# Six weight blocks transposed by DMA instead of TensorE and VectorE, in a kernel whose order of work is a written table

## Chip, core and metric

The kernel runs on one core of a Trainium2 chip. The metric is the device time of one launch in microseconds (us): the median of three runs before the change is 213.56 us (213.39 to 213.92). The engines of a core work side by side and meet only through semaphores: TensorE (PE in the profile), VectorE (DVE), ScalarE (ACT), GpSimd (POOL), and SyncE (SP), which here issues nearly all the DMAs.

## Reference, cut to what matters

Chunk-selecting attention over 4 batches of 8 heads (768 positions, 64 per head), followed by a gated MLP block with a matrix `w_sg` (768x768) that mixes positions:

```python
h = x @ w_in                                   # x: attention's output, 768 x 512 per batch
h = gelu(h)
u, v = h[..., :512], h[..., 512:]
v_n = (v - mean(v)) / sqrt(var(v) + 1e-6) * g_ln
v_s = einsum('ts,bsd->btd', w_sg, v_n) + b_sg[None, :, None]
return x + (u * v_s) @ w_out
```

The sum over `s` needs `w_sg` with `s` on the partitions, that is, transposed.

## The kernel before, in words

`_build` makes a list of steps with `P.op` (lines 57 to 98): each has an engine, a function that emits its instructions, an estimated cost, the names that it reads and writes, and a tag. Dependencies follow from the names. The steps are numbered in the order in which they are made. `TABLE` then says for each engine in which order its steps run ("pe", "act", "dve", "pool", "sp"), and in "slots" which PSUM buffer each PSUM tile gets. An engine runs its list strictly in order: a step that waits holds up everything behind it on that engine. That holds for SP too, where the steps are DMA issues.

The tags used below: for a pair of heads p, `kn_p`, `qn_p`, `vn_p` load k, q and v (lines 528, 537, 543); `ktr_p`, `qtr_p` transpose k and q on PE, half by half (L550); `kmm_p` takes minima and maxima of chunks on DVE (L578); `kev_p`, `qev_p` move the transposed halves out of PSUM (L450 on ACT, L453 on DVE); `rel_p` is a ReLU of q (L616, L619), `qcast_p` and `vcast_p` are casts on POOL. `ub_p` scores the chunks on PE (L660, L707); `utr_p`, `m8_p`, `dn_p`, `dt_p` on DVE make the selection, which `qd_p` copies by DMA to the rows of QA (L740). `sc_p` are the attention scores on PE, `exp_p` their exponentials on ACT, `aff_p` the causal mask on POOL, `pv_p` and `pvd_p` the products with v on PE, `rcp_p` and `xs_p` the normalization on DVE into XS.

After each four pairs a batch b is complete. `xtr_b` transposes a 128-column block of XS on PE and `xev_b` copies it into xT (in batch 0 on ACT, L450); in batches 1 to 3 three of the four blocks are transposed by DMA, `xtd_b` (L906). Then `hv_b` (L943) and `hu_b` (L962) are the products with `w_in` on PE, `gv_b` and `gu_b` the GELUs on ACT, `bns_b`, `bna_b`, `var_b` the statistics on DVE, `rstd_b` the power on POOL (L984), `vhat_b` the normalized v on DVE (L996), `pt_b` the product with the transposed `w_sg` on PE (L1014), `vs_b`, `gt_b` on DVE, `ou_b` the product with `w_out`, `os_b` and `st_b` the addition and the store.

`wsg_load(j)` handles a row block of `w_sg`, 128 rows by 768 columns: `ws_j` loads it in fp32 to one of four staging buffers (name `stg`, j mod 4); `wsc_j` casts it on POOL to bf16 into one of four buffers (`stb`, j mod 4) that lie in the memory of `vhat` of batch 0; `wst_j` is six PE transposes of 128x128 into PSUM (L496); `wev_j` is a DVE copy from PSUM into `wsgT` (L453). Since the buffers lie in `vhat`, no `vhat_0` may start before the last `wst_j` has read them. `ws_5` overwrites the staging buffer of `ws_1` and waits for `wsc_1`; `wsc_4` and `wsc_5` overwrite the buffers that `wst_0` and `wst_1` read.

Of the kernel before, what the change touches and what calls it, by code (L numbers as in the profile page):

```python
# [260 lines left out]
def _build(nc, ctx, q, k, v, w_in, g_ln, w_sg, b_sg, w_out, out):  # L261
# [4 lines left out]
    NT = S // 128  # L266
# [54 lines left out]
    KSPR = 8  # L321
    GTP = ()
    WSB = 1
    WSC = "pool"
    OSV = 1
    OSPL = 1
# [150 lines left out]
    def wsg_load(j):  # L477
# [4 lines left out]
        if WSB:  # L482
            sb = vh0[:, S * (j % 4):S * (j % 4) + S]
            if WSC == "pool":
                cast(sb, dst, S, ("wsc", j), [("stg", j % 4)] + names, [("stb", j % 4)])
            elif WSC == "dve":
                P.op("dve", lambda d: d.tensor_copy(sb, dst), dve(S, rate=2), ("wsc", j), port=True,
                     reads=[("stg", j % 4)] + names, writes=[("stb", j % 4)])
            else:
                P.op("act", lambda d: d.activation(sb, dst, ACTF.Copy), act(S), ("wsc", j),  # L490
                     reads=[("stg", j % 4)] + names, writes=[("stb", j % 4)])
            t = ps_g.tile((0, 1))

            def trb(e, t=t):
# [617 lines left out]
    for p in range(4, NP + 4):  # L1112
# [19 lines left out]

TABLE = {
# [19 lines left out]
    "act": (  # L1153
# [11 lines left out]
    "dve": (  # L1165
# [18 lines left out]
    "pool": (  # L1184
# [13 lines left out]
    "slots": (  # L1198
        "0123021232033001111103211301001112301011000111023013323000101132100111010012301010102132032123220323"
        "3232223333321100112210110011102310011001101032100001100132100101110303223203321332233232232221011013"  # L1200
        "2101000001132101010001011330110001110220111010032103310123213323323223233201011032010011320001112311"
        "010022012320013111020122002331032103"),
    "filler": (
        "45:7 54:4 84:4 "),
}


# [57 lines left out]
```

## Time and profile before

| | us |
|---|---|
| median of three runs | 213.56 |
| profiled execution, its own time | 213.85 |
| span of the profiled execution, first to last instruction | 212.1 |
| TensorE busy, share of the span | 203.4, 96% |
| VectorE busy | 184.1, 87% |
| ScalarE busy | 158.5, 75% |
| GpSimd busy | 88.8, 42% |

The profile is of one execution. Its views: the page (busy times, slices of the span, the chain of work that ended last), groups of instructions by line and shape, timelines of one engine, sums over windows, and the DMAs with the time from issue to landing. In a timeline a row is a start, a length, the engine, the line, the operation with its tiles, and how many like instructions were merged into it. Busy times of PE overlap, since matmuls are pipelined: what a matmul costs the next one is the distance of their starts, not its own length.

### The profile page before, as it was taken

The page shows a single profiled execution, that of the slowest core. Times are in us where ns is not written, and L with a number is a line of the kernel's source. Part 1 is how long each engine was busy: PE and PEld are TensorE (multiplying, and loading weights), DVE is VectorE, ACT ScalarE, POOL GpSimd, SP SyncE. Part 2 cuts the span into 40 slices and gives each one's busy share as a digit, 9 for nine tenths or more (in the row PEclk, how much of TensorE's full clock was granted, in tenths as well). Part 3 has the DMA queues.
Part 4 walks back from the last instruction along what each step waited for, and adds up shares of the span by engine and source line. Part 5 has one row for each costly group of instructions (what it writes and reads, how often), then busy time and mean ns, then how long its engine had stood idle before and what let it go on. Part 6 is the DMA issues. An engine that isn't in the chain of part 4 may idle for free.

```text
span 212.1 us, 5923 instructions
## 1 busy us (share of the span) xinstructions
PE 203.4 (96%) x2326; PEld 134.0 (63%) x2326; DVE 184.1 (87%) x537; ACT 158.5 (75%) x246; POOL 88.8 (42%) x119
## 2 busy tenths in 40 slices
PE   7989999889999999999999999999999999999993
PEld 3646677644767577776456767779646668545552
DVE  2999999879999899898799999899897887788894
ACT  2468999987599779998949989999977868256000
POOL 8424697795262645474121456465502311002000
PEclk9999999999999999999999999999999999999999
DMA  7999999992989998898989988826320007412007
GB/s 152 218 219 254 212 237 336 338 306 68 221 225 231 215 273 205 194 211 189 230 201 220 207 165 220 224 79 149 59 61 3 3 0 97 129 47 105 2 33 264
DMA packets 91339, 36.07 MB, mean 170 GB/s; under 512 B 84144, under 2 KB 86448, under 8 KB 91312
## 3 DMA queue, kind: packets, MB, share of 16 engines
q1 hardware_dynamic: 91024, 35.31, 73.7%
q8 instruction: 18, 0.29, 0.6%
q10 hardware_dynamic: 288, 0.39, 0.5%
q14 instruction: 9, 0.07, 0.1%
HBM read 24.77 MB, written 6.29 MB: 146 GB/s over the span
## 4 chain that ended last, share of the span: by engine, by line
PE 63%; DVE 23%; ACT 9%; issue 2%; POOL 1%; DVEq 0%
PE PSG L1014 15%; PE PSC L795 11%; PE PSG L1047 9%; PE PSG L943 7%; DVE W L578 6%; PE PSG L962 6%; ACT E L801 5%; PE PSG L550 5%; PE PSG L879 4%; DVE vhat L996 3%; DVE XS L897 2%; PE PSG L707 2%; ACT KA L450 2%; PE PSC L382 2%; PE PSG L885 2%
## 5 line engine op out<-in xcount | busy, mean ns | idle before, releaser
L801 ACT ACTIVATE E<-PSC 128x1024 bf16<-128x1024 f32 (+1 forms) x72 | 62.9, 917 | 7.8 <-PE PSC L795 7.6
L795 PE MATMUL PSC<-QA,KA 128*128 128x128 bf16 (+2 forms) x336 | 37.5, 246 | 0.4
L578 DVE TENSOR_REDUCE W<-PSG 128x12 f32<-128x384 f32 x64 | 32.7, 547 | 3.8 <-PE PSG L550 3.6
L1014 PE MATMUL PSG<-wsgT,vhat 128*128 128x384 bf16 x192 | 34.5, 326 | 0.4 <-DVE vhat L996 0.2
L806 POOL TENSOR_SCALAR_AFFINE_SELECT E<-E 128x768 bf16<-128x768 bf16 x24 | 21.1, 878 | 32.3 <-ACT E L801 31.9
L625 POOL CAST QA<-qT 64x768 bf16<-64x768 f32 (+1 forms) x28 | 24.1, 859 | 15.9 <-ACT qT L450 10.0
L795 PEld LDWEIGHTS PSC<-QA,KA 128*128 128x128 bf16 x336 | 24.1, 98 | 8.4 <-ACT E L801 2.4
L1014 PEld LDWEIGHTS PSG<-wsgT,vhat 128*128 128x128 bf16 x192 | 17.9, 98 | 12.5 <-ACT uT L968 1.3
L1047 PE MATMUL PSG<-woutb,uT 128*128 128x512 bf16 (+1 forms) x100 | 23.7, 371 | 0.0
L962 PE MATMUL PSG<-xT,winb 128*128 128x384 bf16 x128 | 23.6, 326 | 0.0
L1031 DVE SCALAR_TENSOR_TENSOR PSG<-PSG,glnT,bsgbc 128x384 f32<-128x384 f32 x32 | 19.7, 619 | 4.1 <-PE PSG L1014 3.9
L849 ACT ACTIVATE E<-PSC 128x1024 bf16<-128x1024 f32 (+3 forms) x26 | 21.2, 866 | 2.4 <-PE PSC L840 2.1
L943 PE MATMUL PSG<-winb,xT 128*128 128x512 bf16 x96 | 22.1, 379 | 0.6 <-issue 0.6
L968 ACT ACTIVATE uT<-PSG 128x384 bf16<-128x384 f32 x32 | 15.1, 490 | 10.0 <-PE PSG L962 9.7
L450 ACT ACTIVATE KA<-PSG 128x384 bf16<-128x384 f32 (+1 forms) x38 | 18.3, 492 | 3.7 <-DVE W L578 3.3
L879 PE MATMUL PSG<-vx,E 128*128 128x65 bf16 x480 | 19.9, 194 | 1.0 <-DVE XS L897 0.6
L635 POOL CAST vx<-vn 128x768 bf16<-128x768 f32 x16 | 13.3, 836 | 17.8 <-DMA vn<-in_v_dram 13.4
L879 PEld LDWEIGHTS PSG<-vx,E 128*128 128x128 bf16 x480 | 17.6, 97 | 3.6 <-DVE XS L897 1.5
L948 ACT ACTIVATE vgb<-PSG 128x512 f32<-128x512 f32 x24 | 13.2, 599 | 7.2 <-PE PSG L943 7.0
L1035 DVE TENSOR_TENSOR uT<-PSG,uT 128x384 bf16<-128x384 f32 x32 | 17.7, 555 | 0.9
L897 DVE TENSOR_TENSOR XS<-PSG,rden 128x384 bf16<-128x384 f32 x32 | 17.7, 554 | 0.9
L952 DVE BATCH_NORM_STATS2 stats<-vgb 128x6 f32<-128x512 f32 x24 | 15.8, 685 | 2.6 <-ACT vgb L948 2.5
(88 smaller groups left out, 328.8 us busy)
## 6 DMA issues: line engine op xcount, KB each, us to landing
kn<-in_k_dram SPq DMA_DIRECT2D x32, 192.0 KB, 4.6
qn<-in_q_dram SPq DMA_DIRECT2D x32, 192.0 KB, 4.5
vn<-in_v_dram SPq DMA_DIRECT2D x12, 384.0 KB, 5.2
out_dram<-osb SPq DMA_DIRECT2D x18, 256.0 KB, 2.4
vn<-in_v_dram SPq DMA_DIRECT2D x8, 192.0 KB, 4.8
uT<-in_moe_w_sg_dram SPq DMA_DIRECT2D x4, 384.0 KB, 6.2
vgb<-in_moe_w_in_dram SPq DMA_DIRECT2D x3, 512.0 KB, 6.1
KA<-INDF SPq DMA_DIRECT2D x12, 96.0 KB, 2.6
```

The costliest lines, as they stand in the source:

```text
L450: P.op("act", lambda e: e.activation(dst(), src(), ACTF.Copy), act(n), tag, reads=reads, writes=writes, ps=ps, shift=shift)
L578: P.op("dve", lambda d, m=m, op=op, src=src, h0=h0, h1=h1: d.tensor_reduce(W[w][:, m, 12 * h0:12 * h1].rearrange("p (h c) -> p h c", h=h1 ...
L625: P.op("pool", lambda g, i=i, r0=r0, r1=r1: g.tensor_copy(QA[w][i or 0][r0:r1, :], qT[r][r0:r1, :]), gps(S, 250 if i == 1 else 150), ("qca ...
L795: r = e.matmul(t.ap()[:, o:o + n], KA[w][i][:, 128 * kb:128 * kb + 128], QA[w][i][:, q0:q0 + n], start=True, stop=True)
L801: P.op("act", lambda e, t=t, c0=c0, c1=c1, i=i: e.activation(E[es][:, i, c0:c1], t.ap()[:, 0:c1 - c0], ACTF.Exp, scale=SCALE), act(c1 - c0 ...
L849: P.op("act", lambda e, t=t, c0=c0, c1=c1, n=n: e.activation(E[es][:, :, c0:c1], t.ap().rearrange("p (i x) -> p i x", i=2)[:, :, 0:n], ACT ...
L879: r = e.matmul(t.ap()[:, 65 * (qb - q0):65 * (qb - q0) + 65], E[es][:, i, at[kb, qb]:at[kb, qb] + 128], vx[w][:, kb, i, :], start=x == 0, ...
L897: P.op("dve", lambda d, pv3=pv3, nq=nq, rs=rs, q0=q0, q1=q1: d.tensor_tensor(XS[:, b % 2, hh // 2, q0:q1, i * DH:(i + 1) * DH], pv3()[:, : ...
L943: r = e.matmul(t.ap()[:, 0:F], xT[s][:, dk, 128 * qt:128 * qt + 128], winb[:, dk, F:DFF], start=(dk == 0), stop=(dk == NDK - 1), skip_grou ...
L962: r = e.matmul(t.ap()[:, 0:TG], winb[:, dk, 128 * fb:128 * fb + 128], xT[s][:, dk, TG * tg:TG * tg + TG], start=(dk == 0), stop=(dk == NDK ...
L1014: r = e.matmul(t.ap()[:, 0:TG], vhat[s][:, sb, 128 * fb:128 * fb + 128], wsgT[:, sb, TG * tg:TG * tg + TG], start=(sb == 0), stop=(sb == N ...
L1047: r = e.matmul(t.ap()[:, 0:n1 - n0], gT[s][:, fb, 128 * qt:128 * qt + 128], woutb[:, fb, n0:n1], start=(fb == 0), stop=(fb == NF - 1))
```

## The change

With `WSD = 1`, `wsg_load` ends after a DMA issued by SP that transposes the bf16 block from its buffer to `wsgT`; the PE transposes, their PSUM tile and the DVE copy are not made:

```diff
+    WSD = 1
@@ wsg_load
+            if WSD:
+                P.op("sp", lambda e: e.dma_start_transpose(wsgT[:, :, 128 * j:128 * j + 128], sb), dmac(1300), ("wst", j),
+                     reads=[("stb", j % 4)] + [("vhat", 0, x) for x in range(NT)],
+                     writes=[("wsgT", j, hf) for hf in range(2)], dma=f"wt{j}", xfer=900)
+                return
             t = ps_g.tile((0, 1))
```

There are six steps fewer on PE (399 instead of 405) and on DVE (403 instead of 409), and six more on SP (182 instead of 176). All five lists and the slots of `TABLE` are new, over the whole kernel. Steps behind the first row block have new numbers. A part of the SP list:

```diff
     "sp": (
...
-        "176 125 78 179 178 72 76 70 239 139 147 235 151 180 143 304 236 300 101 301 305 298 302 102 303 306 "
...
+        "170 173 134 172 78 72 76 146 136 133 143 137 140 233 148 145 294 229 230 142 139 296 102 297 292 101 "
```

Written with tags, from the 38th step of SP on, up to which both lists have issued the same loads in other orders, with kn_6 standing for one load of each of its two heads (kn_6a, kn_6b):

```
SP before: ... wi_0 vn_5 ws_2 ws_4 kn_6a ws_5 wo_0 ws_3 qn_7a kn_6b qd_5a wb qd_5b qn_7b qd_4a kn_7a wg kn_7b vn_6 ...
SP after:  ... wi_2 ws_5 wst_1 wst_0 ws_4 ws_2 ws_3 vn_5 wst_5 wst_4 qd_5a kn_6a kn_6b wst_3 wst_2 kn_7a wg kn_7b qd_4a wb qn_7b ...

POOL before: ... aff_2 aff_2 mrow_2 vcast_3 wic_3 aff_3 aff_3 wic_1 qcast_5 wic_2 wic_0 qcast_5 vcast_5 mrow_3 wsc_2 wsc_4 wsc_5 woc_0 wsc_3 rstd_0
POOL after:  ... aff_2 aff_2 vcast_3 wsc_1 aff_3 aff_3 mrow_2 wic_3 mrow_3 wic_1 wic_2 qcast_5 wsc_5 qcast_5 wsc_4 wsc_2 wsc_3 vcast_5 rstd_0

ACT before:  ... exp_3 (last) kev_5 qev_5 kev_5 kev_5 rel_5 xev_0.2 xev_0.1 xev_0.0 xev_0.3 gv_0 ...
ACT after:   ... exp_2 (last) xev_0.0 exp_3 ... exp_3 (last) qev_5 kev_5 x4 rel_5 xev_0.2 xev_0.1 xev_0.3 gv_0 ...

DVE before, second selection: dt_0 kev_2 rel_1 kmm_2 kev_2 kmm_2 init kmm_2 kmm_2 utr_1 m8_1 qev_2 dn_1 wsub_2 dt_1 qev_3
DVE after, second selection:  dt_0 kmm_2 wsub_1 rel_1 kmm_2 qev_2 kev_2 kmm_2 kmm_2 utr_1 m8_1 init wsub_2 kev_2 dn_1 qev_3 dt_1
DVE before, batch 0: ... dn_4 bns dt_4 ... bns wev_4 wev_5 bna bna var wev_3 kmm_6 kmm_6 wev_2 vhat x6 kmm_6 kmm_6
DVE after, batch 0:  ... dn_4 dt_4 bns ... bna bna var kmm_6 kmm_6 kmm_6 vhat kmm_6 vhat x5

PE before: ... xtr_0.1 xtr_0.2 ub_4 xtr_0.0 xtr_0.3 hv_0 ... wst_4 wst_5 hu hu wst_3 ktr_6 hu hu wst_2 hu hu sc_5 qtr_7 hu hu qtr_7 hu sc_4 ktr_6 pt_0
PE after:  ... xtr_0.0 (among the scores of pair 2) ... xtr_0.2 xtr_0.1 ub_4 xtr_0.3 hv_0 (24 matmuls) and hu_0 (31 of 32) ktr_6 hu sc_5 ktr_6 sc_5 sc_5 ktr_7 ktr_7 pt_0
```

In the lists before, `wst_0` and `wst_1` stand among the scores of pairs 1 to 3, `ws_0` and `ws_1` are issued among the loads of pairs 0 to 2; after, `ws_0` and `ws_1` are issued some ten places later. In the rest of the kernel (batches 1 to 3) the steps are the same, in another order.

More of the change, by code (lines that the diff above doesn't have):

```diff
@@ L1134 @@
     "pe": (
[18 rows of a table removed]
-    "act": (
[11 rows of a table removed]
-    "dve": (
[18 rows of a table removed]
-    "pool": (
[13 rows of a table removed]
[18 rows of a table added]
+    "act": (
[11 rows of a table added]
+    "dve": (
[17 rows of a table added]
+    "pool": (
[14 rows of a table added]
     "slots": (
[L1199 to L1202, printed above, removed]
+        "0132103022013220313200100113201010110100123012323010010032010111110003201011011021033030132232222233"
+        "3322320011012210101010013300111000111032101101100132110101001033221230213323332332223320101013210100"
+        "1011132100010011001221011001110331001101122003333001213232232323323301101123001100320111103210001022"
+        "012310202101201031112003221302"),
     "filler": (
-        "45:7 54:4 84:4 "),
+        "45:7 56:4 80:4 "),
 }
```

116 rows, old and new, of the table TABLE are left out of this document.

## The prediction

> **What bounds the kernel now.** I read first the page, then windows over three stretches, then the timelines around the places where the removed steps stood.
>
> ```profile
> span 212.1 us, 5923 instructions
> PE 203.4 (96%) x2326; PEld 134.0 (63%) x2326; DVE 184.1 (87%) x537; ACT 158.5 (75%) x246; POOL 88.8 (42%) x119
> DMA  7999999992989998898989988826320007412007
> ...
> PE 63%; DVE 23%; ACT 9%; issue 2%; POOL 1%; DVEq 0%
> ```
>
> The next rows are windows: busy us of PE, PEld, DVE, ACT, POOL, then the granted clock, DMA share and GB/s.
>
> ```profile
> 5.00:25.00 20.00, 18.97 (x250) 12.48 (x249) 19.03 (x66) 13.82 (x23) 9.36 (x16) 1.00 1.25 224
> 25.00:43.00 18.00, 16.83 (x348) 12.92 (x346) 16.74 (x48) 17.61 (x29) 14.13 (x18) 1.00 1.06 299
> 60.00:203.00 143.00, 141.82 (x1549) 94.34 (x1548) 125.81 (x355) 112.63 (x171) 51.98 (x61) 1.00 0.66 144
> ```
>
> Three regimes: until 25 DVE is full (19.03 of 20 us); from 25 to 43 ACT is (17.61 of 18), with DVE close behind; from 60 to 203 PE is (141.82 of 143). The clock is full. In the last regime the order can hardly matter unless it stalls PE: it has the same matmuls before and after. So what decides is when the first `pt_0` starts, what PE has done by then, and whether the new order stalls PE later.
>
> **What is removed.** Six times six transposes and a copy:
>
> ```profile
> 26.43 0.50 PE L496 MATMUL PSG<-identB,vhat 128*128 128x128 bf16 x6
> 26.76 0.34 PE L885 MATMUL PSG<-vx,E 128*128 128x65 bf16 x6
> ...
> 54.23 1.02 DVE L453 COPY wsgT<-PSG 128x768 bf16<-128x768 bf16 x2 [0.42 <-PE PSG L496]
> 55.17 0.24 DVE L954 BATCH_NORM_AGGREGATE mv<-stats 128x2 f32<-128x6 f32 x2
> 55.44 0.17 DVE L982 TENSOR_SCALAR rstd<-mv 128x6 f32<-128x6 f32 x1
> 55.55 0.56 DVE L453 COPY wsgT<-PSG 128x768 bf16<-128x768 bf16 x1
> 56.03 1.01 DVE L578 TENSOR_REDUCE W<-PSG 128x12 f32<-128x384 f32 x2
> 56.96 0.55 DVE L453 COPY wsgT<-PSG 128x768 bf16<-128x768 bf16 x1
> 57.42 2.82 DVE L996 TENSOR_SCALAR vhat<-vgb,mv,rstd 128x512 bf16<-128x512 f32 x6
> ```
>
> PE goes on 0.33 us after a `wst` began (26.43 to 26.76): six are 2.0 us of PE, two of them before 43 where PE isn't the bound, four (1.3 us) in batch 0. A copy costs DVE about 0.46 (the second of the pair at 54.23 ends 1.02 after the first began): 2.8 us in all, two copies before 43, four before `vhat_0`. These 1.3 us of PE are the most obvious gain; if all else stayed, 212.1 would become 210.8.
>
> **What is added.** Six DMA transposes on SP. The same shape, 128x768 bf16 from SBUF to SBUF, is there nine times as `xtd`; I take its rows (launch time, its place in the span, then landing):
>
> ```profile
> L906 SPq DMA_TRANSPOSE xT<-XS x9: 1212/1278/2717, 92.0 to 178.4; - x9
> DMA to landing us min/median/max: 2.8/2.9/4.9
> ```
>
> So 1.28 us of SP each (up to 2.72) and 2.9 us to landing (up to 4.9). The destination differs, 128-element pieces in rows of 768, but 256-byte pieces either way; I take the median and keep the longest for the range. The Trainium skill (VectorE: DVE Perf Modes, "The three transpose paths") speaks against the change: it gives 1309 ns for a 128x128 block by the DMA crossbar against 390 ns on TensorE. By it, if blocks followed one another, a row block of six would take an estimated 7.9 us; the trace's 2.8 to 4.9 for six blocks disagrees, and the row decides.
>
> What waits behind them on SP, in the new list: `ws_5` and `wst_1` wait for `wsc_1`, with five loads behind; `wst_5` and `wst_4` for POOL's casts; then `qd_5` for `dt_4`, and only then `kn_6`, `wst_3`, `wst_2`, `kn_7`. Before, `kn_6` and the like were out by 44:
>
> ```profile
> 42.68 1.65 SPq L528 DMA_DIRECT2D kn<-in_k_dram  x1
> 50.01 0.61 SPq L740 DMA_DIRECT2D QA<-Dt  x1
> ...
> DMA to landing us min/median/max: 2.8/4.6/7.6
> ```
>
> (the last row is of all `kn` loads). The queues were busy up to 48 anyway (the DMA line of the page, a slice is 5.3 us, has nines to its ninth digit), so the first SP wait starves nothing; the price falls behind 50.
>
> **What moves, and the sum.** *ACT, before `hv_0`.* In the second selection `dt_1` now has one more copy of q in front of it (`qev_3`, 0.47 by the pitch of such copies):
>
> ```profile
> 19.93 0.98 DVE L453 COPY qT<-PSG 128x384 f32<-128x384 f32 x2
> ...
> 20.79 1.02 ACT L849 ACTIVATE E<-PSC 128x1024 bf16<-128x1024 f32 x1 [0.62 <-PE PSC L840]
> ...
> 42.13 0.68 ACT L616 ACTIVATE rT<-qT 128x576 f32<-128x576 f32 x1
> 43.24 1.51 ACT L450 ACTIVATE xT<-PSG 128x768 bf16<-128x768 bf16 x2 [0.43 <-PE PSG L919]
> 45.15 1.51 ACT L450 ACTIVATE xT<-PSG 128x768 bf16<-128x768 bf16 x2 [0.40 <-PE PSG L919]
> ```
>
> The exponentials that wait for it (20.79, after 0.62 of idling) start 0.47 later, and from there ACT is dense to `rel_5`, which also gets `xev_0.0` (0.75) ahead of it. So `rel_5`, which ended at 42.81, ends at 44.0. Its successor `ub_4` and two `xev` (1.51) follow: `hv_0` can start at about 45.5, against now:
>
> ```profile
> 43.47 0.72 PE L707 MATMUL PSG<-qT,W 64*32 64x288 f32 x16 [0.26 <-DVE XS L897]
> ...
> 46.06 1.70 PE L943 MATMUL PSG<-winb,xT 128*128 128x512 bf16 x7 [0.61 <-issue]
> ...
> 55.35 0.51 PE L550 MATMUL PSG<-identF,kn 128*128 128x128 f32 x3
> ...
> 56.68 0.81 PE L962 MATMUL PSG<-xT,winb 128*128 128x384 bf16 x4
> ...
> 60.38 0.81 PE L1014 MATMUL PSG<-wsgT,vhat 128*128 128x384 bf16 x4 [0.21 <-DVE vhat L996]
> ```
>
> Here two copies less on DVE before 43 (about 1.0 us, and 0.3 waiting for PE) buy nothing, since ACT has taken over; the bounds of this start are 44.0 (ACT on time, the relief passed on) and 46.5 (ACT another us late); I take 45.5, nearest to the dense row.
>
> *Batch 0, to the first `pt_0`.* From `hv_0` PE has 24 matmuls at 0.22 ((1.70 - 0.38)/6, 0.38 being one's length) and 31 at 0.16 ((0.81 - 0.33)/3): 10.2 us to the first `ktr_6`, so 55.7. DVE's order is `var_0`, three `kmm_6`, a `vhat_0`, the last `kmm_6`, five `vhat_0`. It is through with `var_0` before that (the last GELU's `hv_0` is done about 6.2 us after 45.5) and then stands waiting for `ktr_6`, whose transposes end 0.5 later, at 56.2. Ten steps at 0.46 (the row of six `vhat`: (2.82 - 0.54)/5) and the rest of the last one end at 60.9; `pt_0` starts 0.14 behind, at 61.05. Now it is 60.38: 0.67 later. PE itself is ready at about 58.5; the freed PE time is spent waiting. In exchange one score step more is done ahead (`sc_5`, 640 columns, 0.27 at 0.16 for 384). Net +0.40.
>
> *The DMAs on this path.* `ub_4` to the end of `dt_4` takes the 6.5 us of now less the `bns` (0.6) that stood before it: 44.0 + 5.9 = 49.9.
>
> ```profile
> 49.22 0.76 DVE L735 STREAM_TRANSPOSE Dt<-Dn 128x576 bf16<-128x576 bf16 x1
> ...
> 49.88 0.82 POOL L446 CAST vhat<-vhat 128x768 bf16<-128x768 f32 x1
> 55.70 1.34 POOL L984 TENSOR_TENSOR rstd<-rstd,neghalf 128x6 f32<-128x6 f32 x1 [5.00 <-DVE rstd L982]
> ```
>
> `qd_5` is issued at 49.9, the `kn_6` loads by 51.7, `wst_3` at 51.7, `wst_2` at 53.0; the casts before them are done about when they are now (49.88). `kn_6` lands at 53.9 to 55.7, needed at 55.7; `wst_2` at 55.9 (57.9 by the longest landing), needed by the first `vhat_0` at 57.6; `kn_7` at 58.3 to 60.1, needed at 60.4. All are hidden, with 0 to 2 us to spare where there were 5 and more. I cost them at nothing; without the cover, each us late is a us of the whole.
>
> *Later.* Two transposes, the `kn_6` pair, one `qn_7` and one `wo` now go through the queues behind 50 instead of before: about six times 0.2 MB at 224 GB/s, 5 us of queue less the idle slice there. Loads up to 100 thus land some 3 us later than before, relative to PE. How many slacks that exceeds I can't read; bounds 0 and 2 us, and I take 0.3, near the low end, as PE waited for such loads in one place only in the old order. Sum for the span: 0.67 - 0.27 + 0.3 = +0.7, 212.8; with the 1.75 that lie around the span, 214.55 for an execution like the profiled one, which stood 0.29 above the median. Forecast 214.3.
>
> **Rivals.** (1) *Faster: ACT isn't late.* The exponentials don't feel `dt_1` and DVE's relief reaches ACT; `hv_0` starts at 44.0, the whole chain to `pt_0` is 1.5 shorter, 212.8. Against: ACT's 17.61 of 18. It decides at 45.1: with an earlier start than that the kernel is faster if nothing happens later. (2) *Break-even:* `hv_0` at 45.0 and no price later, 213.5. (3) *A DMA on the path is late:* `kn_6`, `kn_7` or `wst_2` needs its longest landing behind the wait for `dt_4`, and `pt_0` starts 1 to 1.5 later, 215.4. For it: the thin margins above. (4) *Loads late in pairs 6 to 10:* 2 us instead of 0.3, 216. (5) *The transposes hold one another up:* each 4.9 us behind the other, so that `wst_2` lands at 61.5 and `vhat_0` with it, 3.9 later, 218. The skill's 7.9 us per row block would point there.
>
> **How the numbers follow.** Forecast (214.3, own range 213.7 to 214.9) 0.36; (1) 0.24; (2) 0.13; (3) 0.15; (4) 0.09; (5) 0.03. Runs of this kernel tell 0.3% (0.64 us) from no change. Faster: nearly all of (1), 0.23. Same: (2) and the lower part of the forecast's range, 0.23. Slower: the rest, 0.54. The range from 212.3 to 216.2 leaves out (5), half of (4) and the best of (1).
>
> **What would show it.** Start of the first `hv_0`: 45.5 (ACT late) or near 44. First `pt_0` near 61, with DVE idle before `kmm_6`, waiting for PE, and PE idle up to 2.5 us in front of `pt_0`, released by `vhat`: right; PE idle in front of `ktr_6` or `ktr_7`, released by a DMA, is rival 3. Landing of the six transposes: near 2.9, or towards 4.9 and more. PE busy from 60 on at 99%, or holes with DMA releasers. I am wrong if `pt_0` starts before 60, or if the difference arises in batches 1 to 3, where I argued that PE alone counts.

## The result, and the profile after

The changed kernel took 216.47 us in the median of four executions (216.13 to 216.83), the kernel before 213.74 beside it (213.39 to 213.94): 1.013 times as long, 95% interval 1.0107 to 1.0153. The forecast was 214.3, its range 212.3 to 216.2. The profiled execution took 216.39, its span 214.7.

The page of the changed kernel, first the span, the busy shares, then the granted TensorE clock and the DMA share by fortieths of the span:

```profile
span 214.7 us, 5825 instructions
PE 202.0 (94%) x2276; PEld 132.9 (62%) x2290; DVE 185.5 (86%) x531; ACT 158.6 (74%) x246; POOL 89.5 (42%) x119
PEclk9999999999969999999999999999999999999999
DMA  7999999998999999999999979876520003302107
```

Two things are new: a 6 in the line of the clock, and a line of DMA that has nines almost without a gap up to its 23rd digit. (PE's busy time counts records, of which 14 are missing here.) The windows that the prediction read, with columns as there:

```profile
5.00:25.00 20.00, 18.71 (x240) 12.22 (x239) 18.78 (x66) 13.68 (x24) 8.35 (x13) 1.00 1.24 214
25.00:43.00 18.00, 16.31 (x346) 12.42 (x343) 16.75 (x44) 17.53 (x29) 15.14 (x19) 1.00 1.08 280
60.00:203.00 143.00, 140.23 (x1520) 94.22 (x1533) 125.37 (x351) 112.20 (x171) 53.24 (x62) 0.99 0.70 155
```

Up to 43 nothing is gained, as forecast: ACT is as full as before (17.53 of 18 us, before 17.61), and `hv_0` starts at 46.07 (before 46.06). What released `ub_4` in front of it is not ACT's `rel_5`, which ended at 43.83, but DVE's writing of XS, 0.55 us later:

```profile
44.38 0.72 PE L713 MATMUL PSG<-qT,W 64*32 64x288 f32 x16 [0.69 <-DVE XS L903]
```

The loss is in the third row, and the places of single steps in the trace put nearly all of it ahead of the MLP of batch 1: `hv_1` starts 2.5 us later than before (102.12 against 99.63), its last GELU ends 2.4 us later, that of `hv_2` 2.9, and the whole ends 2.5 us later.

PE around the first `pt_0` (timeline: start, length, engine, line, operation, then in brackets the idle time before it and what ended it):

```profile
57.17 0.60 PE L801 MATMUL PSC<-QA,KA 128*128 128x384 bf16 x4
59.31 0.62 PE L801 MATMUL PSC<-QA,KA 128*128 128x128 bf16 x7 [1.54 <-ACT E L807]
60.56 1.29 PE L556 MATMUL PSG<-identF,kn 128*128 128x128 f32 x6 [0.62 <-ACT KA L451]
61.64 2.76 PE L1020 MATMUL PSG<-wsgT,vhat 128*128 128x384 bf16 x8
```

`pt_0` starts at 61.64 (before 60.38, forecast 61.05). PE stands for 1.54 us, because the third of three score steps put in a row needs a PSUM slot (one of the buffers that PE writes its products to) that `exp_5_0_2` frees, and then for 0.62, because `ktr_7` needs the slot that the key copies of pair 6 free. ACT and DVE at that place:

```profile
55.46 1.79 ACT L974 ACTIVATE uT<-PSG 128x384 bf16<-128x384 f32 x4 [0.16 <-PE PSG L968]
57.26 1.28 ACT L807 ACT_TABLE_LOAD   x1
58.56 0.70 ACT L807 ACTIVATE E<-PSC 128x640 bf16<-128x640 f32 x1
59.16 1.73 ACT L451 ACTIVATE KA<-PSG 64x384 bf16<-64x384 f32 x4
```

```profile
56.60 1.49 DVE L584 TENSOR_REDUCE W<-PSG 128x12 f32<-128x384 f32 x3 [0.51 <-PE PSG L556]
58.01 0.54 DVE L1002 TENSOR_SCALAR vhat<-vgb,mv,rstd 128x512 bf16<-128x512 f32 x1
58.46 0.55 DVE L584 TENSOR_REDUCE W<-PSG 128x12 f32<-128x384 f32 x1
58.93 2.36 DVE L1002 TENSOR_SCALAR vhat<-vgb,mv,rstd 128x512 bf16<-128x512 f32 x5
```

DVE does what was forecast, in the order that was forecast; its last `vhat_0` ends at 61.29, but `pt_0` comes 0.35 us behind it and not 0.14, since PE is still at `ktr_7` (the row at 60.56). On ACT, the switch from the GELU table to the exponential's (1.28 us) stands in front of the first exponential, for which PE's first wait is.

The clock, in windows of 3.41 us laid so that the middle one is the stretch with half clock:

```profile
57.46:60.87 3.41, 1.24 (x14) 0.73 (x11) 3.41 (x9) 3.39 (x6) 0.07 (x1) 1.00 0.84 196
60.87:64.28 3.41, 3.41 (x15) 1.90 (x13) 2.43 (x5) 2.92 (x5) 0.87 (x1) 0.50 1.12 250
64.28:67.69 3.41, 3.41 (x29) 2.38 (x28) 3.22 (x7) 1.88 (x3) 1.40 (x2) 1.00 0.90 227
```

PE is busy 1.24 of 3.41 us, and in the next 3.41 us it gets half its clock: 15 matmuls where the window behind it has 29. All four executions have a mean clock of 0.989 to 0.992, those of the kernel before 0.997 to 1.0. The added transposes, last, their time on SP and to landing:

```profile
L494 SPq DMA_TRANSPOSE wsgT<-vhat x6: 1254/1370/1889, 38.4 to 54.0; - x6
...
DMA to landing us min/median/max: 2.8/3.5/4.7
```

### The profile page after: what moved, and what is told of

It reads as the page before. It is cut to its first block, busy times and chain, and to the rows that moved or that the text cites. A ratio compares the mean times of both kernels' runs of the same rounds, so it can differ in the third digit from the quotient of the medians.

```text
span 214.7 us, 5825 instructions
## 1 busy us (share of the span) xinstructions
PE 202.0 (94%) x2276; PEld 132.9 (62%) x2290; DVE 185.5 (86%) x531; ACT 158.6 (74%) x246; POOL 89.5 (42%) x119
## 4 chain that ended last, share of the span: by engine, by line
PE 64%; DVE 23%; ACT 8%; issue 1%; POOL 1%; DVEq 0%
PE PSG L1020 15%; PE PSC L801 11%; PE PSG L1053 9%; PE PSG L556 7%; PE PSG L885 5%; DVE W L584 5%; PE PSG L968 5%; PE PSG L949 5%; DVE stats L958 3%; DVE vhat L1002 3%; ACT E L807 2%; PE PSG L713 2%; PE PSC L383 2%; DVE XS L903 2%; PE PSG L891 2%; ACT KA L451 2%
## 5 line engine op out<-in xcount | busy, mean ns | idle before, releaser
L1020 PE MATMUL PSG<-wsgT,vhat 128*128 128x384 bf16 x192 | 36.1, 335 | 0.5 <-DVE uT L1041 0.3
L1020 PEld LDWEIGHTS PSG<-wsgT,vhat 128*128 128x128 bf16 x192 | 18.4, 100 | 12.9 <-issue 1.9
L974 ACT ACTIVATE uT<-PSG 128x384 bf16<-128x384 f32 x32 | 14.6, 492 | 13.4 <-PE PSG L968 13.2
L968 PE MATMUL PSG<-xT,winb 128*128 128x384 bf16 x128 | 23.1, 326 | 0.0
L1053 PE MATMUL PSG<-woutb,uT 128*128 128x512 bf16 (+1 forms) x90 | 21.7, 369 | 0.6
L949 PE MATMUL PSG<-winb,xT 128*128 128x512 bf16 x92 | 21.4, 379 | 0.3
L968 PEld LDWEIGHTS PSG<-xT,winb 128*128 128x128 bf16 x128 | 12.4, 98 | 9.3 <-ACT uT L974 0.5
```

Source lines behind the costliest of these rows:

```text
L949: r = e.matmul(t.ap()[:, 0:F], xT[s][:, dk, 128 * qt:128 * qt + 128], winb[:, dk, F:DFF], start=(dk == 0), stop=(dk == NDK - 1), skip_grou ...
L968: r = e.matmul(t.ap()[:, 0:TG], winb[:, dk, 128 * fb:128 * fb + 128], xT[s][:, dk, TG * tg:TG * tg + TG], start=(dk == 0), stop=(dk == NDK ...
L1020: r = e.matmul(t.ap()[:, 0:TG], vhat[s][:, sb, 128 * fb:128 * fb + 128], wsgT[:, sb, TG * tg:TG * tg + TG], start=(sb == 0), stop=(sb == N ...
L1053: r = e.matmul(t.ap()[:, 0:n1 - n0], gT[s][:, fb, 128 * qt:128 * qt + 128], woutb[:, fb, n0:n1], start=(fb == 0), stop=(fb == NF - 1))
```

## The experiments

Sixteen kernels ran. The kernel before ran beside each series: medians of 213.79 (first four), 213.70 (e5 to e8), 213.79 (e9 to e11), 213.81 (e12 to e14), 213.68 (e15, e16).

### PE kept busy in the wait: e1, e2

```
-                    for (o, n, kb, q0) in mms:
+                    for (o, n, kb, q0) in mms * {(5, 0, 1): 4}.get((p, i, c), 1):
```

(e2: `{(5, 0, 1): 4, (5, 0, 0): 2}`.)

> The changed kernel, with the score group sc_5_0_1 issued four times in place of once (the same products into the same PSUM, so the result is unchanged); it ends as late as before sc_5_0_0 could start, and its reader exp_5_0_1 comes two steps later on ACT. It fills the 1.54 us in which PE waits at 57.77 and leaves the 0.62 us before 60.56. Clock theory (the waits in front of the first token-mixing group halve the granted clock from 60.87 for 3.41 us, worth about 1.6 us): mean clock back from 0.992 to 0.999, 214.9 us, if the first wait alone is to blame; half clock and 216.4 if the second wait is enough by itself. Rival (the loss lies in the new order or in late loads behind 60): 216.4 whatever the clock does, because the filled time was idle. Rival (the transposes themselves): 216.4.

> As e1_fill_first, with sc_5_0_0 issued twice as well, which fills most of the second wait; exp_5_0_0 starts at 60.91 behind the key copies of pair 6 on ACT and is not delayed. Clock theory: no stretch below full clock, 214.9 us (216.47 less about 1.6). Rivals as for e1_fill_first: 216.4.

Measured: e1 216.16 us (215.54 to 217.63), clock 0.998 to 1.0 in each execution; e2 took 215.49, 216.07, 218.71 and 219.02, clock 1.0. The clock came back as expected, the time did not. PE of e1, at the wait and 20 us later (the execution with the profile is the slowest of the four, 217.63):

```profile
57.50 1.91 PE L801 MATMUL PSC<-QA,KA 128*128 128x384 bf16 x16
59.64 0.62 PE L801 MATMUL PSC<-QA,KA 128*128 128x128 bf16 x7 [0.23 <-ACT E L807]
60.88 0.93 PE L556 MATMUL PSG<-identF,kn 128*128 128x128 f32 x6 [0.62 <-ACT KA L451]
61.68 1.64 PE L1020 MATMUL PSG<-wsgT,vhat 128*128 128x384 bf16 x9
```

```profile
77.97 1.03 PE L1053 MATMUL PSG<-woutb,uT 128*128 128x512 bf16 x4
80.19 0.52 PE L556 MATMUL PSG<-identF,qn 128*128 128x128 f32 x3 [1.19 <-issue]
```

With full clock, the third group of `pt_0` starts at 64.36, 1.25 us ahead of the changed kernel's 65.61. At 79.0 PE stops for 1.19 us in front of `qtr_10`. The row names no releaser, but the trace has the second load of `qn_10` issued at 74.32 and landed at 80.10; after it the lead is gone. The profile of e2 (the execution of 216.07) has the same in two smaller pieces:

```profile
79.11 0.52 PE L556 MATMUL PSG<-identF,qn 128*128 128x128 f32 x3 [0.16 <-issue]
114.63 0.52 PE L556 MATMUL PSG<-identF,qn 128*128 128x128 f32 x3 [0.79 <-ACT uT L974]
```

The q loads in question landed at 79.02 and 114.54 (the second row names ACT, but its wait ends with the landing). So the clock theory is right in its mechanism and wrong as the whole: what the full clock gains, about 1.2 us, PE loses again to late loads, 1.2 in e1 and 0.95 in e2. In the profile of the changed kernel no wait of PE behind 60 names a load; e6 below bears that out.

### The transposes without the new order, and the new order with its chain shortened: e3, e4

e3 has the order of the kernel before, without the PE transposes and the copies. On SP (tags in place of numbers):

```
- ws_5 wo_0 ws_3 qn_7_0 kn_6_1 qd_5_0 wb_0 qd_5_1 qn_7_1
+ ws_5 ws_3 wst_0 wst_1 wo_0 qn_7_0 kn_6_1 wst_2 wst_4 wst_5 qd_5_0 wst_3 wb_0 qd_5_1 qn_7_1
```

> The DMA transposes alone: the order of the kernel before on every engine, the six transposes of PE and the six copies of DVE struck out, the six DMA transposes put on SP (blocks 0 and 1 behind the load of w_sg block 3, which goes ahead of wo_0; blocks 2, 4, 5 ahead of qd_5_0, block 3 behind it). If the transposes are harmless and the new order is what costs: PE is full from 46 to 60 in the kernel before and four of its transposes lie there at 0.33 us each, so the first token-mixing group starts 1.3 us sooner: 212.4 us, clock 0.999. If the transposes themselves cost (DMA, SP): not below 213.7. Clock theory adds a condition: where the freed time turns into a PE wait of over a microsecond in front of the token mixing, the clock drops there too and 1.3 us gained becomes 0.3 us lost (214.0).

Measured: 218.90 us (217.64 to 220.26), clock 0.984 to 0.992. The transposes are not harmless in the old order; they cost 5 us there, as I had placed them, half clock included.

```profile
56.19 0.60 PE L801 MATMUL PSC<-QA,KA 128*128 128x384 bf16 x4
59.83 0.55 PE L556 MATMUL PSG<-identF,qn 128*128 128x128 f32 x3 [3.04 <-DMA qn<-in_q_dram]
```

PE is done with `sc_5_0_1` 1.1 us sooner than before and then waits 3.04 us for `qn_7_1`, which came behind all six transposes on SP (issued at 55.98, before at 51.83). Half clock follows. The new order, which loads `kn_7` and `qn_7` late but uses them late as well, avoids this: it is the better order for DMA transposes.

e4 is the changed kernel with PE, DVE and ACT each reordered in one place:

```
PE  - sc_5_0_0 ktr_7_0 ktr_7_1 pt_0_0_3 pt_0_0_0
    + sc_5_0_0 pt_0_0_3 pt_0_0_0 ktr_7_0 ktr_7_1
DVE - kmm_6_0 vhat_0 kmm_6_0 five vhat_0, kmm_7 x3, vs_0 gt_0 vs_0 gt_0 kmm_7
    + six vhat_0, kmm_6_0 x2, vs_0 gt_0 vs_0 gt_0 kmm_7 x4
ACT - kev_6_1 kev_6_0 kev_6_0 kev_6_1 exp_5_0_0
    + kev_6_1 kev_6_1 exp_5_0_0 kev_6_0 kev_6_0
```

> The changed kernel with DVE's six vhat_0 ahead of kmm_6_0, and the first two token-mixing groups ahead of ktr_7 on PE (their followers on DVE and ACT moved to match). The first group can start when the vhats end, about 60.5 in place of 61.64, and the 1.54 us wait at 57.77 stays. Clock theory: if 1.54 us alone halves the clock, it is halved again and the gain is the 1.0 us of the earlier start: 215.4; if only both waits together do, the clock stays full and it is 213.8. Rival (loads or order behind 60): 216.4 less nothing, since later steps would wait anyway.

Measured: 217.20 us (216.20 to 217.86), not better. The profiled execution (216.88) started `pt_0` at 59.39 and had half clock from 59.18 to 62.59; later PE waits 1.0 us for key copies on ACT.

### Light loads: e5, e6, e7

The loads of q and k of pairs 8 to 11 bring 128 of their 768 rows; the other rows keep what an earlier pair left, and the heads of these pairs come out of other numbers.

```
-                j0, j1 = 3 * h0, 3 * h1
+                j0, j1 = 3 * h0, 1 if 8 <= p <= 11 else 3 * h1
```

on the kernel before (e5), on the changed one (e6), and on e2 (e7).

> The kernel before, with the 16 loads of q and k of pairs 8 to 11 cut to one sixth of their rows (the other rows keep what an earlier pair left, so the heads of these pairs come out of other numbers); 2.6 MB less go through the DMA queues between 60 and 95. It is the base for the next two. DMA theory (between 50 and 100 the DMA queues are full, and what is put into them comes out as PE time): the kernel before waits for a DMA itself in one place, hv_1 for xtd_1_2 at 99.63, so 213.1 to 213.6. Rival (DMA has slack there): 213.7, unchanged.

> The changed kernel with the same 16 loads cut. DMA theory: the late loads behind 65 go away, but half clock from 60.87 for 3.41 us stays, since the waits before it have to do with ACT and DVE: about 1.0 us better than the changed kernel, 215.5 (base plus 1.0 for the first token-mixing group starting later, plus 1.6 for the clock). Clock theory alone: 216.4, unchanged.

> The changed kernel with the same 16 loads cut and the score groups sc_5_0_1 four times and sc_5_0_0 twice, as in e2_fill_both: no late loads and no half clock. If the loss is half clock plus DMA lateness that hide one another (e1 and e2 gained 1.4 us by the full clock up to 67 and stood waiting for qn_10 at 79), both removed together give the base plus the 1.0 us of the later start: 214.2, with a spread as small as before's. If neither is the cause: 216 or more, as e1 and e2.

Measured: e5 213.99 (213.38 to 214.20), the same as before (1.0008, 0.9995 to 1.0020); e6 216.35 (214.16 to 217.11); e7 215.00 (214.64 to 215.30), 1.0064 (1.0046 to 1.0081), clock 1.0. The four cells belong together: taking away the half clock alone (e2) or the late loads alone (e6) does not lower the median clear of noise, taking away both lowers it by 1.47 us (the changed kernel less e7).

The traces show how. By the places of ACT's steps, e6 runs 0.3 us ahead of the changed kernel from 49.5 to the end: with half clock, the light loads give nothing. e2 is 0.4 ahead at 49.5, 1.2 at 66 and 0.3 from 120 on. e7 is 0.5 ahead at 49.5, 1.4 at 66, and keeps it to the end. What they are ahead by at 49.5 comes before anything that the edits touch and is scatter, so by the traces the two together are worth 0.9 us, by the medians 1.47.

What is left with both gone, 1.3 us (e7 less 213.70), I put down to `pt_0`, which starts at 61.52 in e7, 1.1 us later than in the kernel before; that is argued, not shown. e6 was expected at 215.5, and its executions scatter over 3 us. The scatter goes with the clock: three with a mean clock of 0.991 or 0.992 took 216.06, 216.65 and 217.11, the one with 0.999 took 214.16, less than any of e7. So the 1.3 us are uncertain as well; by this one execution 0.5 would be left.

### What a DMA transpose costs by itself: e8, e13, e10

e8 adds this to the whole kernel before; on SP one of the five stands ahead of `wo_0`, four behind `kn_7_1`:

```
+    for j in range(5):
+        dd = uT[1][:, j, :].rearrange("p (a x) -> p a x", x=128) if j < 4 else DUM[:]
+        P.op("sp", lambda e, dd=dd: e.dma_start_transpose(dd, winb[:, 3, 0:S]), dmac(1300), ("dum", j),
...
```

e13 changes the issue to

```
-e.dma_start_transpose(dd, winb[:, 3, 0:S])
+e.dma_start(dd, IND[:].rearrange("p a b -> p (a b)").rearrange("p (a x) -> p a x", x=256)[:, :, 0:128])
```

> The kernel before, whole, with five more DMA transposes of 128x768 bf16 that nobody reads (one on SP ahead of wo_0, four behind kn_7_1_0, into memory that is free then): the suspected cost of the change alone, without its gain and without its order. DMA theory: the loads behind them come some 5 us later on SP, the slacks read in the trace of before (vn_6 1.0, wo_1 0.3, qn_10_0 2.4, mrow_1_1 2.7, xtd_1_2 0.05) are used up: 215 to 217.5. Rival (the queues have room for them): 213.7.

> As e8_dummy_before, with five plain DMA copies from SBUF to SBUF in place of the five transposes: the same bytes in the same pieces of 256 bytes, on the same places of SP. By the share of queue time (the six transposes of the changed kernel added 9.0 us of 16 engines, 1.5 each; what else goes over that queue takes 4.4 us a MB, 0.87 for as many bytes) a copy costs 0.58 of a transpose: 4.0 x 0.58 = 2.3, 216.0. If the bytes decide: 217.7, as e8. If it is the transpose as such, which holds SP for 1.3 us: 213.7 to 214.5.

Measured: e8 217.69 us (217.02 to 218.22), 1.0189 (1.0162 to 1.0215): 4.0 us for five transposes that nothing waits for. e13 216.88 (216.33 to 218.79), 1.0158 (1.0116 to 1.0200): 3.1 us for five copies. This is the clearest row of the study: the same work on PE, DVE, ACT and POOL, in the same order, and 1.9% lost. SP and PE of e8:

```profile
54.31 0.66 SPq L529 DMA_DIRECT2D kn<-in_k_dram  x1
55.02 6.02 SPq L1115 DMA_TRANSPOSE uT<-winb  x4
61.09 0.58 SPq L538 DMA_DIRECT2D vn<-in_v_dram  x1
```

```profile
65.32 0.61 PE L796 MATMUL PSC<-QA,KA 128*128 128x128 bf16 x7
67.61 0.60 PE L796 MATMUL PSC<-QA,KA 128*128 128x384 bf16 x4 [1.68 <-DMA QA<-Dt]
```

`vn_6` is issued at 61.09 where it was at 55.02. Behind it the trace has load after load landing just as it is wanted: `qd_4_1` at 67.52 (its scores at 67.61), `qn_6` 71.49 (71.85), `mrow_1_1` 76.69 (76.95), `qn_10` 79.25 (79.34, after a wait):

```profile
79.34 0.52 PE L551 MATMUL PSG<-identF,qn 128*128 128x128 f32 x3 [0.92 <-DVE U L717]
```

In the kernel before, these four had 2.4 to 3.5 us to spare. In e13 the four copies hold SP for half as long, yet the same loads have only 0.05 to 0.7 us to spare, and later ones are waited for:

```profile
54.39 3.02 SPq L1115 DMA_DIRECT2D uT<-IND  x4
```

```profile
96.37 0.61 PE L796 MATMUL PSC<-QA,KA 128*128 128x128 bf16 x7 [1.86 <-ACT E L802]
```

(The row names ACT, whose exponential was over by then; the DMA `mrow_3_1`, which these scores need as well, landed at 96.28.) So neither SP's time per transpose nor transposing as such explains most of the cost: plain copies of the same 0.2 MB each, at the same places, push what is behind them nearly as far. Which measure of the queue it goes by stays open: by the profile pages' shares of engine time (73.7% of 212.1 us before, 76.9% of 216.2 in e8, 73.8% of 215.4 in e13) the copies added 2.7 us of 16 engines and the transposes 10.0, and e13 should have cost 1.1 us.

e10: the same five transposes, into E[0], on SP directly behind `kn_6_1`.

> As e8_dummy_before (the kernel before, whole, with five DMA transposes that nobody reads), but all five lie on SP behind kn_6_1, in the 5.7 us in which SP waits for dt_4. DMA theory: about 1 us of SP is left over, the loads behind come 1 us later, and slack takes most of it: 213.9 to 214.8, clearly under the 217.7 of e8. If a transpose costs 0.8 us wherever it is (contention, memory port): 217.7 again.

Measured: 219.01 us (218.78 to 220.45), worse than e8, against my expectation.

```profile
44.61 9.38 SPq L1117 DMA_TRANSPOSE E<-winb  x5
54.04 0.61 SPq L740 DMA_DIRECT2D QA<-Dt  x1
```

SP was idle there, the queue behind it was not: the first transpose was held on SP for 4.05 us and landed after 6.06, behind loads that landed up to 50.09. The five took 9.38 us instead of 6.5, `qd_5_0` came at 54.04 for 50.01, `qn_7_1` landed at 61.43, and PE stood 3.58 us for it, with half clock for 6.83 us after.

### The dose: e9, e11, e12

All three have the order of the kernel before, but on SP, from `ws_4` or `kn_6_1` on (the order of the loads differs too, so the three are not doses of one thing alone):

```
e9  + wst_0 wst_1 ws_5 ws_3 wo_0 kn_6_0 qn_7_0 kn_6_1 qn_7_1 kn_7_0 kn_7_1 wst_2 wst_4 wst_5 qd_5_0 wst_3 qd_4_0 wb_0 wg_0 qd_5_1
e11 - if WSD:
    + if WSD and j >= 2:
    + kn_6_1 qn_7_1 kn_7_0 kn_7_1 wst_2 wst_4 wst_5 qd_5_0 wst_3 qd_4_0 wb_0 wg_0 qd_5_1
e12 - if WSD:
    + if WSD and j in (2, 4):
    + kn_6_1 wst_2 wst_4 qd_5_0 wb_0 qd_5_1 qn_7_1
```

> As e3_dma_old_order (the order of the kernel before, six DMA transposes), but SP's idle time from 44.3 to 50 is used for loads that need nothing of batch 0: qn_7_1 and both kn_7 go ahead of the transposes of blocks 2, 4, 5, 3, blocks 0 and 1 go ahead of ws_5, kn_6 behind them, and qd_4_0 is ahead of wb_0. DMA theory: what waited in e3 (qtr_7_1 for qn_7_1 at 59.8, 3.0 us, and half clock after it) is gone, PE gains its 1.3 us before the token mixing, and what is left of some 8 us of SP for six transposes after 5.7 us of idling makes the loads behind 53 about 2 us later than before: 212.4 if their slack holds that, 213.6 if half of it comes out. If six transposes cost the same wherever they are: about 218, as e8 and e3.

> The order of the kernel before, with blocks 2 to 5 transposed by DMA and blocks 0 and 1 left on PE and DVE, where PE isn't the bound; SP's order from 44.3 as in e9 (qn_7_1, kn_7, then blocks 2, 4, 5, qd_5_0, block 3). 2.6 us less of SP than e9, the same 1.3 us of PE gained: 212.4 to 213.0 by the DMA theory. If the gain of PE is no gain (something else sets the first token-mixing group): 213.7.

> The order of the kernel before, with blocks 2 and 4 alone transposed by DMA (on SP behind kn_6_1 and ahead of qd_5_0), the other four on PE and DVE. The dose between 0 (213.7) and 4 (e11: 215.5) and 6 (e9: 219.6). Queue theory: each transpose takes 1.3 to 1.5 us of a queue that is full until 49.4 and idle only from there to 52; two just fit, PE gains 0.66: 213.3 to 214.0. If a DMA transpose costs 0.8 us wherever it is, less 0.33 of PE each: 214.6.

Measured: six by DMA 219.64 (219.51 to 219.97), four 215.52 (214.58 to 217.22), two 213.70 (213.21 to 214.23; 0.9992, 0.9981 to 1.0003), none 213.8. In e9 PE waits 2.29 us for `qd_5_0`, now the one behind the transposes, and 2.68 in front of `pt_0` for `vhat_0`, which waited for block 3 to leave the staging memory that it is written to (landed 60.19, first `vhat_0` 60.27); half clock follows. In e11 PE reaches the first `pt_0` 1.3 us sooner and waits 1.20 for `vhat_0`, again behind block 3 (landed 56.50, first `vhat_0` 56.59). e12 is the clean case: no wait in front of `pt_0`, which starts at 59.49, 0.9 us sooner than before, and the exponentials of pair 7 are still 0.8 ahead at 96. Then, on PE:

```profile
99.77 1.47 PE L949 MATMUL PSG<-winb,xT 128*128 128x512 bf16 x6 [0.82 <-DMA xT<-XS]
```

`hv_1` waits for `xtd_1_2`, which lands when it did before (99.72; before 99.58). PE's gain is real, and in this execution (214.23, the slowest of twelve) the DMA chain takes it back.

### All three suspected causes away; the DMA chain shortened: e14, e15, e16

e14 is e4 with e1's filling and the light loads for pairs 7 to 11. e15 is e12, and e16 the kernel before, with this on SP:

```
- kcp_9 st_0_5 qn_12_1 xtd_1_0 xtd_1_1 st_0_4 xtd_1_2 kin_9
+ qn_12_1 xtd_1_0 xtd_1_1 xtd_1_2 st_0_5 kcp_9 st_0_4 kin_9
```

> The changed kernel with all three suspected causes taken away: the order of e4 (vhat_0 ahead of kmm_6_0, two token-mixing groups ahead of ktr_7), the 1.54 us wait filled as in e1, and the loads of q and k of pairs 7 to 11 cut to one sixth of their rows (these heads come out of other numbers). If later start, half clock and late loads are the whole loss: 213.5 to 214.0, the time of the kernel before. If one is missing: 214.5 or more.

> e12_two_by_dma with two stores and kcp_9 moved on SP from in front of xtd_1_0 and xtd_1_2 to behind xtd_1_2, 1.8 us of SP. In e12 the first token-mixing group started at 59.49 (before 60.38) and PE was 0.8 ahead up to 96, and then stood 0.8 us in front of hv_1, which waits for xtd_1_2. If the DMA chain in front of hv_1 is what takes the gain back: 213.0, 0.8 under the kernel before. If PE would wait at hv_1 or behind it for something else: 213.7.

> The kernel before with the same move on SP alone, as a control. In its trace PE is busy up to hv_1 at 99.63, xtd_1_2 lands at 99.58: nothing to gain, 213.7 to 213.8. If the DMA chain was a bound there already: 213.0 to 213.5.

e14 measured 215.96 us (215.70 to 216.15), clock 0.998 to 1.0: worse than e7.

```profile
59.84 2.12 PE L1020 MATMUL PSG<-wsgT,vhat 128*128 128x384 bf16 x12 [0.52 <-DVE vhat L1002]
...
66.39 0.55 PE L556 MATMUL PSG<-identF,qn 128*128 128x128 f32 x3 [0.98 <-ACT KA L451]
```

`pt_0` starts at 59.84, 0.5 sooner than in the kernel before, but the order that allowed this puts the key copies of pair 7 late on ACT, and PE stands 0.98 and 0.36 us in front of `qtr_7` and its scores. So e14 made a new wait, and whether the 1.3 us left in e7 are the later start alone isn't shown.

e15 measured 214.16 us (213.25 to 215.41; 1.0026, 1.0007 to 1.0044), e16 214.27 (213.51 to 215.41; 1.0028, 1.0015 to 1.0040). In the profiled execution of e15 the wait is gone and `hv_1` starts 0.9 sooner than before:

```profile
98.77 2.50 PE L949 MATMUL PSG<-winb,xT 128*128 128x512 bf16 x10
```

and that one execution took 213.71. Over twelve executions of e15 and eleven of e16 the move on SP costs 0.3% in both kernels and doubles their scatter; why, the single profiles don't show. No version was found that beats the kernel before.

## Why the prediction was wrong, point by point

**Where PE's gain would go** was right in that nothing is gained up to `hv_0`: `rel_5` ends at 43.83 (forecast 44.0), `hv_0` starts at 46.07 (45.5, bounds 44.0 to 46.5). That ACT alone is the bound there was not: `ub_4` waited for DVE (XS) up to 44.38, and `hv_0` came 0.57 later than forecast.

**The start of `pt_0`** had the right sign; DVE waited for `ktr_6` and then did its ten steps in the order named. The size was 1.26 where +0.67 was written. Of the 0.59 missing, 0.4 came through `hv_0` and `ktr_6` (at 56.08, forecast 55.7) to the last `vhat_0` (61.29, forecast 60.9). The other 0.2 are PE's: it was at `ktr_7`, which had waited for ACT and partly ran at half clock, and not idle in front of `pt_0` as forecast.

**"PE itself is ready at about 58.5; the freed PE time is spent waiting"** is the step that failed. PE was ready at 57.8 and did wait, 2.2 us in two pieces; the wait was costed at nothing, and the sentence "The clock is full" was read from the kernel before and carried over. PE got half its clock for the next 3.41 us, and the third group of `pt_0` came 1.25 us later than with full clock (e1). The first piece of the wait had an owner that I never priced: the score slot that waits for the first exponential behind a table load of 1.28 us. The later start (1.26) and the half clock (1.25) are 2.5 us, as much as the span grew, before the score step done ahead (forecast at 0.27) is taken off.

**"Later", 0.3 with bounds 0 and 2**, cost about nothing in the profiled execution of the changed kernel, by luck: PE that is slowed by the clock reaches the loads late. With full clock 0.3 is too little: e1 loses 1.2 us at one load, e2 0.95 at two, and e8 and e13 show what 1 MB more in the queues costs by itself in the old order, 3 to 4 us. The prediction counted the queue's bytes and left the loads' slack as "I can't read"; it could be read, load by load, as landing against first use.

**The DMAs on the path** were right: `kn_6` landed by 55.3, `wst_2` at 56.9, `kn_7` at 59.6, all in time, so rival 3 did not happen in this order (in e3, e9 and e10 a DMA on the path was late, though another one). Rival 5 neither: 3.5 us to landing, at most 4.7. The estimate of 7.9 us a row block by the Trainium skill's figure (VectorE: DVE Perf Modes, "The three transpose paths") is not borne out in this run either. Rival 4 gave nearly the right time, 216, but by luck: its late loads cost time only where the half clock is away. Rivals 1 and 2 needed an earlier `hv_0`, which did not come.

**That PE alone counts from 60 on** holds only while loads are early. Before the change PE was busy 141.82 of 143 us with loads whose slack in front of `hv_1` was 0.05 us.

## What to carry to other kernels

Work moved from a busy engine to DMA is not free because its own result is hidden: price the transfers queued behind it, each by its landing against its first use, and treat an idle issuing engine as free only if the landings show that the queue behind it is empty. A wait that seems to cost nothing on a matmul engine is also a question to the clock: sum PE's idle time over a few microseconds, not wait by wait. And where removing one cause changes nothing, remove two together before dropping either.

## What the runs showed of the hardware that was not expected

The clock is granted in steps of one length on a grid. In every profiled execution that lost it, full clock lasted a whole number of times 3.413 us (54.61 = 16 x 3.413; e9 58.03 = 17 x 3.413) and half clock 3.41 us, or 6.83. The first record of the clock begins between 4.6 and 7.3 us into the span, differently in each execution. Windows laid on this grid, for e4, e8, e10 and e13 in this order; the row behind a window has the clock that followed it:

```profile
55.76:59.18 3.42, 1.57 (x17) 0.99 (x14) 3.42 (x8) 3.38 (x6) 0.39 (x1) 1.00 0.78 179
59.18:62.59 3.41, 3.20 (x11) 1.52 (x12) 1.08 (x3) 2.91 (x4) 0.87 (x1) 0.50 1.01 227
```

```profile
65.03:68.44 3.41, 1.73 (x18) 1.26 (x17) 2.89 (x6) 2.21 (x5) 1.71 (x3) 1.00 1.18 227
68.44:71.85 3.41, 3.41 (x31) 2.40 (x30) 2.37 (x5) 2.94 (x5) 1.18 (x2) 1.00 1.23 246
```

```profile
57.29:60.70 3.41, 0.65 (x6) 0.25 (x3) 2.96 (x7) 1.23 (x3) 0.00 (x0) 1.00 0.79 157
60.70:64.11 3.41, 2.59 (x11) 1.90 (x12) 0.00 (x0) 0.89 (x2) 0.00 (x0) 0.50 0.87 207
64.11:67.53 3.42, 3.42 (x15) 2.00 (x14) 1.02 (x2) 3.24 (x6) 2.56 (x4) 0.50 0.90 236
```

```profile
93.46:96.88 3.42, 1.56 (x31) 1.32 (x28) 2.07 (x14) 2.17 (x5) 1.06 (x2) 1.00 1.11 228
96.88:100.29 3.41, 3.11 (x59) 2.81 (x57) 2.58 (x6) 3.17 (x5) 2.54 (x4) 1.00 1.25 205
```

A window with PE busy 0.65 (e10), 1.24 (the changed kernel) or 1.57 us (e4) was followed by half clock, one with 1.56 (e13) or 1.73 (e8) was not; at half clock, 2.59 us busy did not bring the full clock back, 3.20 and 3.41 did. Busy time alone thus doesn't sort the windows near 1.56 us, and why e4's and e13's differ stays open. That a wait of 1.54 us can cost or not by where the grid lies fits e4: three of its executions had a mean clock of 0.989 to 0.992 and took 216.88 to 217.86, one had 1.0 and took 216.20. Where the grid lay in that one is not on record. The Trainium skill (TensorE: Matmul & The Clock Gate, "Part 1: The HAM clock gate") gives a free-running window of 3413 ns, which these rows bear out. Its advice to avoid idle gaps of over some 3 us ("Why this matters for your kernels") is too mild by them: gaps of 1.54 and 0.62 us in one window were enough.
